# Modulation gates as columns through DRAM, grouped DMA transposes and a new order in an adaLN block

## The chip, the cores and the metric

The kernel runs on one core of one Trainium2 chip. The metric is the device time of one execution in microseconds (us). Engines are named as in the profile: PE (TensorE), PEld (its weight loads), DVE (VectorE), ACT (ScalarE), POOL (GpSimd) and SP (SyncE, which here only issues DMAs).

## The reference

One transformer block with conditioning: a linear attention with a Hedgehog feature map, and a gated feed-forward part. S = 2048 tokens, D = 512, 32 heads of 16, F = 1376; all inputs are bf16.

```python
mod = (silu(c) @ w_mod).reshape(6, 512)          # c: (1, 512), w_mod: (512, 3072)
sa, ca, ga, sb, cb, gb = mod
h = layernorm(x) * (1 + ca) + sa
q, k, v = h @ wqkv                                # 32 heads of 16
phi(t) = [softmax(t @ w_phi), softmax(-t @ w_phi)]   # 32 features a head
kv, z = phi(k).T @ v, phi(k).sum(tokens)          # per head
o = (phi(q) @ kv) / (phi(q) @ z + 1e-6)
x = x + ga * (o @ wo)
h = layernorm(x) * (1 + cb) + sb
x = x + gb * ((sigmoid(h @ w_gate) * (h @ w_up)) @ w_down)
```

The six vectors of `mod` do not depend on the token. `ga` and `gb`, the gates, scale the columns of `wo` and `w_down`.

## The kernel before, in words

The 2048 tokens are 16 tiles of 128 (t = 0 to 15). All weights and x stay in SBUF. The program is a graph of some 1200 small tasks. Each task has a name, the engines it can run on, and a function that issues its instructions. A text, `ORDER`, lists all tasks in one sequence that was searched ahead of time; `@A`, `@D`, `@P` choose ACT, DVE or POOL where the first engine given for the task is not meant. Every engine runs its tasks in the sequence of that text, and waits only for data and for buffers. Buffers are given out along the same text. PSUM has 8 banks.

The names that matter (numbers are tiles or parts):

- `ld_*`: loads, all issued by SP. `ld_wm00`, `ld_wm01`, `ld_wmga`, `ld_wmm2` load w_mod in pieces; `ld_x0a` to `ld_x3` load x.
- `c1`, `c2`, `c3`: silu(c) as a column. `warm0`, `warm1_*`: matmuls on zeros, to fill PE's early waits.
- `modc1`, `modc2` (line 723; copies at 728 and 729): shift and scale of the two LayerNorms as columns: 128 x 1 matmuls with w_mod as the weights, one for each 128 outputs and each quarter of the 512 inputs.
- `scb` (693): silu(c) spread over 128 columns. `ga`, `gb` (901): the gates as 128 equal rows, by 4 matmuls of 512 columns each. `gac` (906) and `gbc` (903): their copies out of PSUM. `wo0` to `wo3` (908) and `wd0` to `wd10` (917): the weights times the gates.
- `tpw`, `wTc`, `wqT`, `fold`, `foldc` (742 to 767): w_phi is folded into the q and k weights; `bd` (694) is the block-diagonal w_phi, and its tile is written again by `perm` (284, 287) with a permutation that `kvp` uses.
- LayerNorm 1: `st1`, `rs1`, `nmr1`, `xn1` (782 to 811) by token tile; then the transpose, in the groups of `LG`. Where `TD` is 0, `tph` (824) transposes on PE into PSUM, and `hm1` (831, 833) applies scale and shift on the way out. Where `TD` is 1, `xT1` (816) transposes by DMA into h1T, and `hm1` works in place.
- For each token tile: `K` (850) and `V` (854) project, `e` (866) takes exp of both signs, `n` (869) sums over the features, `r` (879 to 882) takes the reciprocal, `phi` (872) multiplies, `va` (890) copies v, and `kv` (274) adds to two PSUM banks over all tiles. `NPART` splits these by parts in the last tiles: `phi14.4` is the part of tile 14 from 4/8 on.
- `kvm` (295), `kvp` (310), `kvz` and `kvn` (319 to 327) turn the sums into one 128 x 144 block for each of 8 groups, kvbd. No output token can be worked on before this; it closes the first stage.
- `Q` (928), `qe` (933): the transposed query features of 4 tiles at a time; they fit in before and behind that point.
- For the output tokens: `sm`, `smS`, `den` (tiles 0 to 7) or `z` (367, 369) and `dn` (383 to 391; tiles 8 to 15): the denominators; `num` (360, 444), `u` (433 to 450), `o` (468), `oT` (471, by DMA; through PE for the first two tiles), `out` (477, with wo), `x1` (482), `st2`, `rs2`, `nmr2`, `xn2`, `xnT`, `mod` (second LayerNorm, 486 to 547).
- The feed-forward part by chunks of 1, 1, 2, 4, 4, 4 tiles: `g`, `u` with a dot (568), `tg` (tanh, 578), `hm` (589), `y` (606), `fin` (613), `st` (615, the store). `y` of tile t takes 11 matmuls, y0.0 to y0.10, and y0.k needs `wd`k. The last tile's y is cut by columns in two pieces, the second marked `b`.
- `bnd*`: a check on the size of the inputs, which chooses a general path that does not run here.

```python
LG = [[0], [1], [2, 3], [4, 5], [6, 7], [8, 9], [10, 11], [12, 13], [14, 15]]
TD = [0, 0, 0, 0, 0, 0, 1, 1, 0]
G.add("scb", {"ACT": 0.62}, lambda e: act.activation(scb[:], sc_bf[:].unsqueeze(2).to_broadcast([P, KT, P]), ACT.Copy), ...)
```

Of the kernel before, what the change touches and what calls it, by code (L numbers as in the profile page):

```python
# [22 lines left out]
NG = 8  # L23
# [7 lines left out]
LG = [[0], [1], [2, 3], [4, 5], [6, 7], [8, 9], [10, 11], [12, 13], [14, 15]]  # L31
TD = [0, 0, 0, 0, 0, 0, 1, 1, 0]
MGU = 5
LETTER = {"A": "ACT", "D": "DVE", "P": "POOL"}
ORDER = """
wdz warm0 c1 warm1_0 warm1_1 warm1_2 pmem ld_x0b st1_3 st1_2 bd c2 rs1_2 warm1_3 ld_x0a st1_0 warm1_4 warm1_5 warm1_6 rs1_0 ld_wk ld_x1 st1_1 rs1_1 warm1_7
tpw3 tpw2 wTc2 tpw0 ld_wm00 ld_wm01 wTc0 tpw1 c3 wTc3@D nmr1_2 warm1_8 warm1_9 warm1_10 warm1_11 warm1_12 warm1_13 xn1_0 nmr1_1 wTc1 fold13 foldc13 xn1_2@P
fold11 fold10 tph03 tph01 fold12 foldc10 foldc11 foldc12 xn1_1@P xn1_3@P st1_5 ld_x2 st1_4 st1_6 st1_7 modc1.0 ld_wv tph02 tph23 tph21 rs1_3@P nmr1_3 modc1.1
modc1c tph20 tph13 warm1_14 tph00 hm1_20 hm1_01@A hm1_21@A hm1_03@A hm1_13 hm1_00 hm1_02 tph22 rs1_4@P nmr1_4 K0 tph10 hm1_22@A hm1_23@A K2 ld_wq st1_11 e0.0
xn1_4@P xn1_5@P xn1_6@P hm1_10@A st1_10 tph11 st1_9 st1_8 e2.0 hm1_11@A tph12 hm1_12@A V2 xn1_7@P tph31 K3 hm1_31 e3.0 tph43 tph30 K1 tph32 rs1_6@P nmr1_6  # L40
# [8 lines left out]
n14.4 Q02 kv11.0 kv11.2 Q11 V13 ld_wg qe02 qe11 scb kv11.6 r14.4 n15.0 va13@D r15.4 n14.0 phi12.0 r14.0 r15.0 phi14.4 V14 V15 va15 va14 phi15.4 ga kv12.0
kv13.0 modc2.0 kv13.4 kv14.4 kv15.4 phi14.0 qe10 Q01 kvm1 gac kvp2 kvz2 kv14.0 phi15.0 kv15.0 qe01 Q32 kvm0 kvp1 kvp0 qe32 wo1@D wo2 kvz0 kvz1 gb kvn1@A kvn2  # L50
sm0 modc2.1 sm1 modc2c smS1 gbc kvn0 smS0@D qe13 Q12 sm2 num00 num21 num31 num01 den0 wo0 wo3 den1 Q21 qe12 smS2 wo_all wmod_free u00 u01 num11 num30 tpo0 oT0
den2 u31 u30 u11 wd4 Q31 qe31 wd0 wd2 o3 out0 num10 num20 Q23 qe21 x1_0 u10 wd7 wd1 Q30 qe23 st2_0 u21 u20 qe30 rs2_0 Q33 tpo1 sm4 smS4 nmr2_0 oT1@D xn2_0
num60 Q22 num71 qe33 den4 xnT0 out1 oT3 out3 Q20 u71 x1_1 u60 mod00@A mod02@A mod03@A mod01@A x1_3 st2_3 g0.9 g0.0 u0.9 g0.6 u0.0 o2 wd9 tsw tg0.9 tg0.0 oT2
out2 hm0.0 qe20 tg0.6 wd5 g0.5 g0.8 u0.6 wr st2_1 hm0.9 hm0.6 tg0.5 tg0.8 x1_2 u0.5 u0.7 u0.8 hm0.5 hm0.8 wd6 wd10 rs2_1 sm3 g0.1 g0.7 num61 u0.1 qe22 nmr2_1
st2_2 tg0.7 tg0.1 hm0.1 u0.4 wd3 g0.3 u0.3 tg0.3 xn2_1 g0.2 g0.10 g0.4 u61 hm0.3 hm0.7 tg0.4 tg0.2 u0.2 y0.0 rs2_2 hm0.2 nmr2_2 y0.1 xnT1 num70 o6 xn2_3@P
y0.2 y0.3 u0.10 wd8 xn2_2@P mod11 oT6 xnT3 xnT2 hm0.4 num50 y0.4 u70 smS3@D y0.5 y0.6 mod10@A tg0.10 mod13@A mod12@A u1.1 g1.1 y0.7 tg1.1 num51 g1.5 hm0.10
den3 hm1.1 g1.8 g1.9 u1.5 tg1.9 tg1.5 u51 u50 hm1.5 y0.8 y0.9 u1.8 y0.10 fin0 u1.4 g1.4 tg1.4 hm1.4 g1.0 u1.9 u1.0 num41 g1.3 num40 tg1.8 hm1.9 hm1.8 tg1.0
u1.6 u1.3 g1.2 u1.7 mod21@A tg1.3 u40 hm1.0 hm1.3 o7 mod20@A g1.6 tg1.2 tg1.6 hm1.6 u41 u1.10 g1.7 tg1.7 u1.2 o5 out6 mod22@A mod23@P g2.2 oT7 o4@D out7 x1_6
hm1.7 hm1.2 st2_6 x1_7 g2.0 g2.6 u2.0 g2.10 tg2.6 st2_7 tg2.0 st0 oT5 oT4 hm2.0 g1.10 u2.10 u2.6 tg1.10 hm2.6 hm1.10 rs2_4 nmr2_4 g2.1 u2.4 g2.4 tg2.10 hm2.10
num80 z80@D xn2_7@D tg2.4 tg2.1 hm2.4 num81 u2.1 hm2.1 num82 y1.0 out5 z81@D tg2.2 z82 dn8 x1_5 u800 y1.1 y1.2 y1.3 u2.2 hm2.2 xn2_6 xnT7 xnT6 y3.0 out4 g2.8  # L60
g2.5 u2.8 y1.4 tg2.5 y1.5 y1.6 y1.7 y1.8 y1.9 tg2.8 st2_5 x1_4 st2_4 u811 u821 hm2.8 u820 g2.7 y3.1 g2.3 u2.5 rs2_3 u2.3 mod43@A tg2.3 nmr2_3 xn2_5 xnT5 hm2.5
xn2_4@P xnT4 hm2.3 y1.10 num102 z102@D fin1 num92 tg2.7 g2.9 u2.9 num91 num90 y2.0 y2.1 y3.2 tg2.9 z91@D hm2.9 z90 z92 dn9 y3.3 y3.4 u2.7 y2.2 y3.5 y2.3 u900
u921 hm2.7 u911 mod40@P y2.4 y3.6 y2.5 num100 num101 y2.6 mod30@A z101 z100 mod31@P mod42@P mod32@P y2.7 st1 u920 num110 y2.8 y3.7 y2.9 y2.10 o9 dn10 u1021
u1000 fin2 u1011 u1020 o10 o8 y3.8 y3.9 mod33@A mod41@A g3.10 g3.8 u3.10 num130 g3.0 y3.10 tg3.10 z130 tg3.8 hm3.10 fin3 st2 oT9 u3.8 num112 hm3.8 tg3.0 z112
# [12 lines left out]
tg5.5 hm5.5 y9.8 y9.9 y9.10 u5.1 u5.0 g5.0 tg5.1 hm5.1 fin11 fin9 u5.9 u5.10 tg5.0 bndc g5.2 hm5.0 tg5.2 u5.4 g5.9 hm5.4 hm5.2 tg5.9 hm5.9 g5.10 st11 st9
tg5.10 hm5.10 bndd y13.0 y13.1 y13.2 y13.3 y12.0 y12.1 y12.2 y13.4 y13.5 y13.6 y13.7 y13.8 y13.9 y13.10 fin13 st13 y12.3 y12.4 y12.5 y12.6 y12.7 y12.8 y12.9
# [1038 lines left out]
```

## Time and profile before

| | |
|---|---|
| median of 3 runs | 210.98 us (210.16 to 211.16) |
| profiled execution | 209.63 us |
| its span, first to last instruction | 207.9 us |
| granted PE clock | 1.00 |
| PE, DVE, ACT, POOL busy | 200.3, 168.2, 107.9, 103.4 us |
| HBM read, written | 11.58 MB, 2.10 MB |
| K0 starts; last `e` ends | 13.35; 50.2 us |
| kvm1, kvm0 start | 55.3, 56.7 us |
| last matmul ends, last add starts | 204.8, 204.84 us |

The median of the runs is the time that is compared. The profile is one execution and has a time of its own; the 1.7 us between its time and its span lie around the instructions. A busy PE may be waiting inside a matmul, because the ends of pipelined matmuls are modelled. A mean duration of an instruction includes what it overlaps with the next one on its engine, so sums of durations come out larger than the time they take.

### The profile page before, as it was taken

To read this page: it belongs to the slowest core of one execution; us is meant where nothing else is said; L and a number is where in the kernel's file an instruction comes from. 1 tells how busy PE (TensorE), PEld (TensorE's weight loads), DVE (VectorE), ACT (ScalarE), POOL (GpSimd) and SP (SyncE) were. 2 spreads that over 40 slices of the span, in tenths; PEclk is the share of its full clock that TensorE was granted. 3 is DMA by queue.
4 is the path that set the end of the run, shared out by engine and by line. 5 is a ranking of instruction groups with operands and counts; after the bars stand their busy time and mean duration, and the time that the engine had idled before them with its cause. 6 is when DMAs were issued, how large, how long until landed. Compare 5 with 4: busy or idle time off the path is not lost.

```text
span 207.9 us, 4302 instructions
## 1 busy us (share of the span) xinstructions
PE 200.3 (96%) x1516; PEld 112.4 (54%) x1539; DVE 168.2 (81%) x459; ACT 107.9 (52%) x259; POOL 103.4 (50%) x137
## 2 busy tenths in 40 slices
PE   7789999999999999999999999999999999999994
PEld 2555465454675588976764544454444444444443
DVE  3999999999599998899988999979797815456642
ACT  2699999999886986524443322521244300142300
POOL 5589999999996989601337202633040612000000
PEclk9999999999999999999999999999999999999999
DMA  6995922999200201522032210342011131001011
GB/s 179 367 349 144 130 32 51 321 390 401 82 3 3 50 2 30 122 33 42 12 76 52 54 25 0 77 101 55 0 29 47 25 79 50 25 2 50 3 60 54
DMA packets 30893, 18.74 MB, mean 90 GB/s; under 512 B 20657, under 2 KB 28818, under 8 KB 30866
## 3 DMA queue, kind: packets, MB, share of 16 engines
q1 hardware_dynamic: 30336, 18.39, 31.6%
q8 instruction: 14, 0.23, 0.5%
q14 instruction: 13, 0.11, 0.2%
q10 hardware_dynamic: 530, 0.02, 0.1%
HBM read 11.58 MB, written 2.10 MB: 66 GB/s over the span
## 4 chain that ended last, share of the span: by engine, by line
PE 74%; ACT 7%; POOL 6%; DMA 4%; DVE 3%; issue 3%; SPq 1%; POOLq 0%; DVEq 0%
PE y_ps L606 18%; PE g_ps L568 17%; PE u_ps L568 17%; PE a_ps L477 6%; POOL phi L872 5%; PE q_ps L928 5%; DMA wmod_sb<-in_w_mod_dram 4%; ACT h1T L831 3%; ACT e L866 2%; DVE ks L869 2%; PE num L360 2%; PE num L444 2%; PE v_ps L854 1%; PE g_ps L570 1%; ACT tg L578 1%
## 5 line engine op out<-in xcount | busy, mean ns | idle before, releaser
L578 ACT ACTIVATE tg<-g_ps 128x512 bf16<-128x512 f32 (+4 forms) x66 | 28.7, 454 | 66.2 <-PE g_ps L568 50.5
L606 PE MATMUL y_ps<-wd_sb,wmod_sb 128*128 128x512 bf16 (+3 forms) x182 | 42.2, 366 | 0.2
L589 DVE SCALAR_TENSOR_TENSOR wmod_sb<-tg,u_ps 128x512 bf16<-128x512 bf16 (+4 forms) x63 | 30.0, 495 | 13.0 <-ACT tg L578 7.0
L872 POOL TENSOR_TENSOR phi<-e,ks 128x1024 bf16<-128x1024 bf16 (+2 forms) x22 | 31.5, 1453 | 0.5
L568 PEld LDWEIGHTS <-wu_sb 128*128 128x128 bf16 (+1 forms) x252 | 21.7, 99 | 15.4
L568 PEld LDWEIGHTS <-wg_sb 128*128 128x128 bf16 (+1 forms) x252 | 21.4, 99 | 15.2 <-issue 0.2
L606 PEld LDWEIGHTS <-wmod_sb 128*128 128x128 bf16 (+1 forms) x187 | 17.9, 98 | 16.5
L568 PE MATMUL g_ps<-wT_sb,wg_sb 128*128 128x512 bf16 (+2 forms) x121 | 23.8, 321 | 0.2
L568 PE MATMUL u_ps<-wT_sb,wu_sb 128*128 128x512 bf16 (+2 forms) x123 | 23.7, 322 | 0.1
L497 POOL TENSOR_SCALAR ve<-mv 128x2 f32<-128x2 f32 (+1 forms) x8 | 1.8, 223 | 41.2 <-DVE mv L487 41.2
L568 PE MATMUL g_ps<-wqk_sb,wg_sb 128*128 128x128 bf16 (+4 forms) x127 | 19.9, 287 | 0.1
L613 DVE TENSOR_TENSOR ot<-y_ps,x 128x512 bf16<-128x512 f32 (+1 forms) x17 | 11.1, 656 | 11.0 <-PE y_ps L606 10.5
L568 PE MATMUL u_ps<-wqk_sb,wu_sb 128*128 128x128 bf16 (+4 forms) x128 | 19.5, 287 | 0.0
L468 POOL TENSOR_TENSOR o<-u 128x512 bf16<-128x512 f32 x12 | 15.2, 1268 | 8.7 <-DVE u L435 4.7
L869 DVE TENSOR_REDUCE ks<-e 128x64 f32<-128x1024 bf16 (+2 forms) x22 | 19.4, 899 | 0.0
L866 ACT ACTIVATE e<-k_ps 128x512 bf16<-128x512 f32 (+2 forms) x44 | 18.1, 502 | 0.3 <-PE k_ps L850 0.2
L933 ACT ACTIVATE eT<-q_ps 128x512 bf16<-128x512 f32 x32 | 17.0, 622 | 1.3 <-PE q_ps L928 1.0
L850 PE MATMUL k_ps<-wqk_f,h1T 128*128 128x512 bf16 x62 | 15.8, 379 | 0.4 <-DVE h1T L833 0.3
L477 PE MATMUL a_ps<-wo_sb,oT 128*128 128x512 bf16 x61 | 15.8, 379 | 0.1
L928 PE MATMUL q_ps<-h1T,wqk_f 128*128 128x512 bf16 x58 | 15.6, 379 | 0.3
L854 PE MATMUL v_ps<-wv_sb,h1T 128*128 128x512 bf16 x62 | 15.6, 379 | 0.2
L782 DVE BATCH_NORM_STATS2 st<-x_sb 128x6 f32<-128x512 bf16 x16 | 10.7, 669 | 2.5 <-DMA x_sb<-in_A_x_dram 2.5
(158 smaller groups left out, 331.3 us busy)
## 6 DMA issues: line engine op xcount, KB each, us to landing
out_dram<-ot SPq DMA_DIRECT2D x15, 128.0 KB, 1.9
x_sb<-in_A_x_dram SPq DMA_DIRECT2D x3, 512.0 KB, 8.5
wmod_sb<-in_w_mod_dram SPq DMA_DIRECT2D x3, 512.0 KB, 7.5
wmod_sb<-in_w_mod_dram SPq DMA_DIRECT2D x1, 1536.0 KB, 14.9
wu_sb<-in_B_w_up_dram SPq DMA_DIRECT2D x1, 1376.0 KB, 9.7
wg_sb<-in_B_w_gate_dram SPq DMA_DIRECT2D x1, 1376.0 KB, 16.4
wd_sb<-in_B_w_down_dram SPq DMA_DIRECT2D x1, 1280.0 KB, 6.6
wqk_sb<-in_A_wqkv_dram SPq DMA_DIRECT2D x2, 512.0 KB, 7.6
```

Of the source, the lines that this page charges most:

```text
L477: pe.matmul(ap_[:], lhsT=oT[:, j, :], rhs=wo_sb[:, j, :], start=(j == 0), stop=(j == KT - 1))
L568: pe.matmul(ps[:fsz, 0:n], lhsT=w[:, j, ft * P:ft * P + fsz], rhs=h[:, j, 0:n], start=(j == 0), stop=(j == KT - 1))
L578: G.add(f"tg{k}.{ft}", {"ACT": 0.13 + n * 0.00083}, lambda e, tg=tg, g_ps=g_ps, fsz=fsz, n=n: act.activation(tg[:fsz, 0:n], g_ps[:fsz, 0:n ...
L589: dve.scalar_tensor_tensor(hm_all[:fsz, hm[k].slot, ft, 0:n], tg[:fsz, 0:n], 1.0, u_ps[:fsz, 0:n], op0=ALU.add, op1=ALU.mult)
L606: mm = pe.matmul(y[:, 0:c1 - c0], lhsT=hm_all[:fsz, hm[k].slot, ft, tl * P:(tl + 1) * P], rhs=wd_sb[:fsz, ft, c0:c1], start=(ft == 0), sto ...
L850: pe.matmul(kp[:], lhsT=h1T[:, j, t * P:(t + 1) * P], rhs=wqk_f[:, j, D:2 * D], start=(j == 0), stop=(j == KT - 1))
L854: pe.matmul(vp[:], lhsT=h1T[:, j, t * P:(t + 1) * P], rhs=wv_sb[:, j, :], start=(j == 0), stop=(j == KT - 1))
L866: act.activation(ee[:, ha:hb, s, :], kp[:, ha * DH:hb * DH].rearrange("p (h j) -> p h j", j=DH), ACT.Exp, scale=1.0 - 2.0 * s)
L869: dve.tensor_reduce(ks[:, ha:hb].rearrange("p h s -> p (h s)"), ee[:, ha:hb].rearrange("p h s j -> p (h s) j"), axis=AX.X, op=ALU.add)
L872: pool.tensor_tensor(ph[:, ha * 32:hb * 32].rearrange("p (h j) -> p h j", j=DH), ee[:, ha:hb].rearrange("p h s j -> p (h s) j"), ks[:, ha: ...
L928: pe.matmul(qp[:], lhsT=wqk_f[:, j, blk * P:(blk + 1) * P], rhs=h1T[:, j, cq * 512:(cq + 1) * 512], start=(j == 0), stop=(j == KT - 1))
L933: act.activation(eT[cq][:, s * 4 + blk, :], qp[:], ACT.Exp, scale=1.0 - 2.0 * s)
```

## The change

1. The gates are worked out as columns, like the shifts and scales: `modca` (16 one-column matmuls) and 16 more in `modc2`; ACT copies them to `gcol`, 128 x 8. SP writes four columns to a DRAM tensor (`gwa`, `gwb`: 512 values of 4 bytes), and reads them back as one row into all 128 partitions (`gra`, `grb`). `scb`, `ga`, `gac`, `gb`, `gbc` and their PSUM banks go.
2. LayerNorm-1 tiles 8 to 15 form two groups of four, both transposed by DMA. `xT1_8`, `9`, `14`, `15` are new, `tph5x` and `tph8x` go; `hm1` of such a group is one instruction of 512 columns for each j, and may run on DVE too.
3. `phi` may run on DVE. `z` copies 16 columns instead of 8 out of PSUM, and `dn` reads only SBUF, with 5 operations fewer.
4. `perm` writes a tile of its own (`bdp`) and no longer waits for the folds.
5. The last tile's y is cut 384 and 128 columns instead of 256 and 256.
6. `ORDER` is another text. The loads keep their sequence up to `ld_x2`; then come wq, wv, wmga, x3, and later wo and wg ahead of the last four transposes. On DVE: phi4.0, 6.0, 11.6, 13.0, 13.4, 14.0, 14.4, 15.4.

```diff
-LG = [[0], [1], [2, 3], [4, 5], [6, 7], [8, 9], [10, 11], [12, 13], [14, 15]]
-TD = [0, 0, 0, 0, 0, 0, 1, 1, 0]
+LG = [[0], [1], [2, 3], [4, 5], [6, 7], [8, 9, 10, 11], [12, 13, 14, 15]]
+TD = [0, 0, 0, 0, 0, 1, 1]
...
+bdp = cst.tile([P, KT, P], BF16, name="bdp")
+gcol = cst.tile([P, 8], FP32, name="gcol")
+gdr = [drp.tile([KT, P], FP32, name=f"gdr{i}") for i in range(2)]
...
-zS = small("smS", [P, 3, 3, 8])
+zS = small("smS", [P, NG, 16])
...
+es = [zS[:, 4 * s:4 * s + 4, 8:16] for s in range(2)]
 for s in range(2):
+    dve.tensor_tensor(m[:, 0, 32 * s:32 * s + 32]..., zS[:, 4 * s:4 * s + 4, 0:8], es[1 - s], op=ALU.mult)
+dve.tensor_tensor(den[:, 0], m[:, 0, 0:32], m[:, 0, 32:64], op=ALU.add)
+dve.reciprocal(den[:, 0], den[:, 0])
+for s in range(2):
+    dve.tensor_tensor(cc[:, 0, s]..., es[1 - s], den[:, 0]..., op=ALU.mult)
...
-steps[-2:] = [(CHUNKS[k] - 1, 0, 256), (CHUNKS[k] - 2, 0, 512), (CHUNKS[k] - 1, 256, 512)]
+steps[-2:] = [(CHUNKS[k] - 1, 0, 384), (CHUNKS[k] - 2, 0, 512), (CHUNKS[k] - 1, 384, 512)]
...
+def f_mc2(ps):
+    act.mul(gcol[:, 4:8], ps[:, 8:12], 0.5)
+    act.copy(modc[:, 8:12], ps[:, 0:4])
+    act.add(modc[:, 12:16], ps[:, 4:8], 1.0)
+modc_task("modca", list(range(8, 12)), ["wmod_ga", "wmod_ga"], ["gcola"], lambda ps: act.copy(gcol[:, 0:4], ps[:]), 0.2)
+modc_task("modc2", list(range(12, 24)), ["wmod_m2", "wmod_m2"], ["mod2", "gcolb"], f_mc2, 0.5)
...
-G.add(f"phi{t}.{a}", {"POOL": 0.08 + 1.77 * w}, f_p, ...)
+G.add(f"phi{t}.{a}", {"POOL": 0.08 + 1.77 * w, "DVE": 0.08 + 1.07 * w}, f_p, ..., port=("POOL", "DVE"))
...
-G.add("gb", {"PE": 0.87}, lambda e: f_mm(e, gb_ps, 5 * D), r=["scb", "wmod_m2"], w=["gb"], bufs=[gb_ps])
-G.add("ga", {"PE": 0.87}, lambda e: f_mm(e, ga_ps, 2 * D), r=["scb", "wmod_ga"], w=["ga"], bufs=[ga_ps])
+def f_gw(i):
+    sp.dma_start(gdr[i][:].rearrange("k p -> p k"), gcol[:, 4 * i:4 * i + 4])
+def f_gr(i):
+    sp.dma_start(gb_bc[:] if i else ga_sb[:], gdr[i][:].rearrange("k p -> (k p)").unsqueeze(0).to_broadcast([P, D]))
```

The new text around the second group's transposes and around the end of the first stage (tasks of other engines in between left out):

```
... ld_wo ld_wg n5.0 xn1_15@D ... xT1_15 phi4.0@D xn1_12@D ... xn1_13 xT1_13 V11 V8 V9 ... gwa ld_wd ... hm1_62@A ... hm1_63@A ... hm1_60@P hm1_61@P K13
... phi15.0 n14.0 r14.4 r14.0 ... phi14.0@D phi14.4@D phi15.4@D V15 perm ... kvm1 ... modc2.0 qe01 qe03 kvm0 kvp2 ... modc2.1 gra wo2 wo0 wo3 ... modc2c ... gwb ... grb
```

More of the change, by code (lines that the diff above doesn't have):

```diff
@@ L37 @@
[L37 to L40, printed above, removed]
@@ L49 @@
[L49 to L52, printed above, removed]
@@ new lines @@
+kv11.6 Q13 r15.4@A va14 qe13 V13 va13 phi14.0@D phi14.4@D phi15.4@D V15 perm Q03 kv12.0 kv13.4 kv14.4 va15 kv15.4 ld_wd2 kvm1 kv13.0 kv14.0 kv15.0 modc2.0
+qe01 qe03 kvm0 kvp2 qe11 wr kvp1 kvp0 modc2.1 gra wo2 wo0 wo3 kvz2 kvz1 kvn1@A modc2c kvn2@A kvz0 sm0 kvn0 smS0@D den0 sm2 smS2 Q30 qe32 den2 num00 qe30 wo1
+wo_all gwb num30 num01 num10 wmod_free Q12 sm1 u01 u00 qe12 smS1 num31 Q23 tpo0 grb u31 den1 u30 oT0 o3 oT3 Q31 num11 out0 u11 x1_0 u10 st2_0 qe31 num20 num21
+qe23 wd4 wd6 Q21 qe21 u20 u21 o2 sm4 oT2 smS4 rs2_0 tpo1 nmr2_0 Q33 Q20 oT1 wd9 wd1 den4 out1 x1_1 num60 num70 xn2_0 xnT0 num71 tsw u70 u60 out3 sm3 num61
@@ L692 @@
     G.add("c3", {"DVE": 0.5}, f_c3, r=["c2"], w=["scbf"], bufs=[c_ps])
-    G.add("scb", {"ACT": 0.62}, lambda e: act.activation(scb[:], sc_bf[:].unsqueeze(2).to_broadcast([P, KT, P]), ACT.Copy), r=["scbf"], w=["scb"])
     G.add("bd", {"POOL": 1.15}, lambda e: pool.tensor_tensor(
@@ L886 @@
             G.add(f"r{t}.{a}", rw, f_r, r=[("ks", t, a)], w=[("kr", t, a)], bufs=[ks])
[L887 removed]
+            G.add(f"phi{t}.{a}", {"POOL": 0.08 + 1.77 * w, "DVE": 0.08 + 1.07 * w}, f_p, r=[("kr", t, a)], w=[("phi", t, a)], bufs=[ee, ks, ph], port=("POOL", "DVE"))
         G.add(f"V{t}", {"PE": 0.87}, f_v, r=h1k + ["wv"], w=[("v", t)], bufs=[vp])
```

155 lines of the change are left out of this document (72 added, 83 removed).

## The prediction

> **What bounds the kernel now.** I read the sums of the page first.
>
> ```profile
> PE 200.3 (96%) x1516; PEld 112.4 (54%) x1539; DVE 168.2 (81%) x459; ACT 107.9 (52%) x259; POOL 103.4 (50%) x137
> ```
>
> PE's 96% says little alone, since a waiting matmul counts as busy. So I priced PE's work by spacings from the chain of waits, where back-to-back work shows what it really takes:
>
> ```profile
> 44.51 0.86 PE k_ps L850 x4
> 57.92 0.86 PE gb_ps L901 x4
> 195.26 9.56 PE y_ps L606 x55
> 204.84 0.42 DVE ot L613
> ```
>
> Four 512-column matmuls take 0.86 us. Priced so, with 0.055 for a 128-column transpose (four take 0.39 in the timeline, less the 0.22 of one alone), the PE tasks of ORDER from the first key projection `K0` (starts at 13.35) to `kvm1` (55.3) sum to 42.05 us in 41.95 us. From there to the last `y` (204.8) they sum to 147.7 in 149.5. PE has no air in the first stage and 1.8 us in the second.
>
> Then the windows (us: busy and count of PE, PEld, DVE, ACT, POOL):
>
> ```profile
> 0.00:13.30 13.30, 10.30 (x102) 5.62 (x102) 9.24 (x31) 7.85 (x20) 8.36 (x30) 1.00 0.88 290
> 13.30:45.00 31.70, 31.34 (x243) 16.77 (x249) 31.34 (x68) 31.50 (x80) 31.05 (x32) 1.00 0.67 178
> 45.00:57.20 12.20, 12.03 (x116) 6.57 (x117) 9.52 (x21) 10.62 (x26) 12.04 (x12) 1.00 0.68 262
> 80.00:130.00 50.00, 49.66 (x397) 32.18 (x402) 46.78 (x159) 18.97 (x54) 17.38 (x23) 1.00 0.22 46
> ```
>
> From 13.3 to 45, DVE, ACT and POOL are as full as PE; to 57 POOL stays full while DVE and ACT get air. From 80 to 130 DVE has only 3.2 us free and POOL is idle two thirds of the time. DVE's own waits from 45 to 58 name what closes the first stage:
>
> ```profile
> DVE kvm L295 <- POOL phi L872: 1.4, 1, 1.4
> ```
>
> **The change, part by part.** Rows used (line, form, count; busy, mean ns):
>
> ```profile
> L901 PE MATMUL gb_ps<-wmod_sb,scb 128*128 128x512 bf16 x4 | 1.0, 380 | 0.0
> L824 PE MATMUL tp_h<-ident,xn 128*128 128x128 bf16 x48 | 5.1, 218 | 0.1
> L723 PE MATMUL modc_ps<-sc_bf,wmod_sb 128*128 128x1 bf16 x64 | 2.2, 163 | 0.1
> L872 POOL TENSOR_TENSOR phi<-e,ks 128x1024 bf16<-128x1024 bf16 x12 | 23.1, 1929 | 0.4
> L908 DVE TENSOR_TENSOR wo_sb<-wo_sb,ga_sb 128x512 bf16<-128x512 bf16 x1 | 0.9, 916 | 0.0
> L450 DVE TENSOR_TENSOR u<-num,cc 128x512 f32<-128x512 f32 x12 | 7.9, 683 | 0.4 <-PE num L444 0.2
> L468 POOL TENSOR_TENSOR o<-u 128x512 bf16<-128x512 f32 x12 | 15.2, 1268 | 8.7 <-DVE u L435 4.7 <-DVE u L450 2.0 <-DVE u L433 1.5
> ```
>
> *Gates on PE.* `ga` and `gb` go: 8 matmuls at 0.216 = -1.73. Tiles 8, 9, 14, 15 lose their PE transposes: 16 at 0.055 = -0.89. Added: 32 one-column matmuls; 16 take 0.54 with 0.16 latency, so 0.025 each = +0.80. PE: **-1.82**, all where PE has no air.
>
> *Gates on ACT.* `scb` 0.72, `gac` 0.62, `gbc` 0.60 go; two copies of 0.17 come: -1.6, beside other work.
>
> *Gates by DMA.* On SP each gate is a write of 512 four-byte pieces, then a read of 2 KB into 128 partitions. No row shows such a write: between 1.9 us (small store) and 3.4 (`wp_sb`, 512 pieces of 32 B); I take 3.4, the nearest row. The read lies between 1.9 and 3.0 (`x_sb`, 256 KB). The ga pair: its read stands on SP behind the loads of wd, wu and the rest of wmod (4.3 MB, 11 us at 390 GB/s); `modc2` needs the same wmod, so it lands before PE gets there, and `wo` starts no later than its 56.3 of before. Nothing. The gb pair comes after `modc2c` (about 57.5): `wd` starts on POOL at 61.3 to 64 where it starts at 60.4 now. SP waits between the pair; behind it stands the transpose `oT3`. `out2` needs o2, behind `wd4` and `wd6`: PE reaches it at about 72, which lets `wd4` start as late as 65.5. Cover 1.5 to 4 us: I take 0; beyond it every us is a us. The Trainium skill (DMA: Bandwidth & Descriptors, Specifications) says that pieces under 512 B are read, modified and written and miss line rate; by it the write alone would lengthen, with no figure for it, and no run here shows such a write.
>
> *LayerNorm 1 in groups of four.* hm1 for tiles 8 to 15 is 8 instructions of 512 columns instead of 16 of 256. 512-column bf16 rows: ACT 0.78 (two xn1 in 1.56), POOL 0.777. The order puts 3 on ACT and 5 on POOL. SP gains four transposes at 1.2 us, and xT1_15, 14, 12, 13 queue behind wo and wg. A transpose lands in 2.4 us, 4.1 to 4.3 behind a load. xT1_13 waits for `xn1_13` on ACT (about 37.6, below), lands at 40 to 42, and K13 follows at about 42: cover 0 to 2 us, and all four tiles must land before the first modulation. I put a loss here into the ACT rival.
>
> *Moves between engines, modc1c to the end of the first stage.* I counted the tasks of both orders, at mean durations. POOL: phi 22 to 14 instructions, hm1 1 to 5, xn1 10 to 7, `perm` later: 44.1 to 32.9. DVE: +8 phi pieces (4.75 full ones), -4 va, -3 foldc, -4 hm1: 46.1 to 46.3. ACT to its last `e`: -3.8 hm1, +1.7 va, +1.7 foldc, +0.8 xn1, +1.1 qe, +0.4 smaller: 42.2 to 44.1. Overlap makes sums of durations too large: DVE's 46.1 took 43.1 less 2.2 idle, a factor 0.89; ACT 0.90.
>
> A full phi on DVE has no row: 1.15 from the reduction of the same 1024 elements (1.195 at L869), 1.83 as twice L908. I took 1.15; the difference is 2.8 us of DVE.
>
> *Startup.* The loads up to wm01 keep their places, so `modc1` still waits for 11.3. But xn1_3 stands on ACT ahead of the four fold copies: 0.78 against 0.43 idle there, `modc1c` slips from 11.97 to 12.25: **+0.28**. Moving wq ahead of wv delays wv by 512 KB (1.5 us, from 14.3 to 15.8); V1 comes at 17. The ga part of wmod ahead of the last x load puts that off as much, to about 20; its statistics come at 28. Nothing.
>
> *dn and z (second stage).* z copies 16 columns instead of 8 and dn runs from SBUF, 5 operations fewer: about -0.6 of DVE for each of 8 tiles. PE is the bound there: 0.
>
> *Tail.* The last piece is 128 columns instead of 256: the final add 0.42 becomes 0.28 (L433's form): **-0.14**; the store lands in 1.9 either way.
>
> Sum: -1.82 + 0.28 - 0.14 = -1.68. Against the profiled execution, 209.63 (span 207.9): 207.95. The median of the runs is 1.35 above it: 210.98 - 1.68 = **209.3**.
>
> **The rivals.**
>
> *More than the sum.* PE's 1.8 us of air in the second stage goes too, since DVE and POOL lose load and the order is new. For: DVE has 3.2 us free in 80 to 130 and gains 4.9. Against: a searched order has no reason to find all of it. 209.3 - 1.8 = 207.5.
>
> *ACT keeps the stage long.* ACT was full from 12.2 to 50.2 and gets 1.9 more (1.7 by the factor), and 0.28 late: its last `e` ends at 52.2. Then n14.0, two reciprocals and three phi halves on DVE (0.65 + 0.7 + 1.95): kvm1 at 55.5, as now; kvm0 at once instead of waiting for POOL, 56.5 against 57.2. PE's work behind that point is the same in both orders (145.9), so PE's saving turns into waiting: -0.65 - 0.14 = -0.8, 210.2. For: the windows. Against: three of those ACT tasks are not needed for K and e to go on.
>
> *POOL's and DVE's port (slower).* The one wo on DVE while POOL does the same work takes 0.916, against 0.683 for 512 elements with an input in PSUM. DVE now gets 48 instructions with both inputs in SBUF (8 phi, 40 in dn) where nearly all read PSUM before. Phi at twice L908: +2.8 us in a stage with 2.2 idle, most of that the wait for phi: +1.2 on the path. If each dn once waits out one `o` of POOL (1.268): 8 x 1.268 = 10.1 less the 4.9 saved = 5.2, less 3.2 free: +2.0. Together +3.2 - 1.68 = +1.5, 212.5. It decides from the point where the waits pass the idle and the saving, 2.2 + 3.2 + 1.7 = 7.1 us, 0.15 us for each of the 48; the wo row shows 0.23 under a full POOL, and POOL is a third full behind 80. The Trainium skill (SBUF — State Buffer, Who interferes with whom) says that such a DVE instruction and a POOL one that reads SBUF exclude each other for a whole instruction: by it the full 1.268 could fall on any of the 48; the row of 0.916 agrees in sign, not in size.
>
> **How the numbers follow.** About 0.5%, 1.05 us, can be told from no change here. Forecast 209.3: 0.36. More: 0.16. ACT: 0.27. Port: 0.21. Faster is the first two, 0.52; same 0.27; slower 0.21. The range runs from 207.0, below the second case, to 212.6, the port at its full price. Within the faster cases alone it is 207.0 to 209.8.
>
> **What would show it.** Right: no ga_ps and gb_ps rows, 32 transposes at tp_h's line, 96 one-column matmuls; kvm1 at 54 to 54.8; the last y about 203.1; the final add 0.28. ACT: `e` ends after 51.5 and key matmuls wait for h1T around 42. Port: phi on DVE over 1.4 for 1024 elements, dn's SBUF operations over their 0.16 to 0.35, DVE above 48 us in 80 to 130. Gates: POOL idle ahead of wd until after 65. I am wrong outright if the startup moves by more than 0.5, or if PE waits in the second stage by more than 3 us.

## The result, and the profile after

| | before | after |
|---|---|---|
| median | 210.57 us (209.77 to 211.16, 4 runs) | 225.99 us (225.23 to 228.76, 4 runs) |
| profiled execution | 209.63 us | 225.23 us |
| its span | 207.9 us | 223.5 us |
| mean granted PE clock | 1.00 | 0.97 |

The changed kernel is slower: 1.0723 times the time before (95% interval 1.0665 to 1.078), 15.4 us. All ratios leave out runs more than 1.5% above the fastest of their kernel; after the change that is the 228.76. Forecast were 209.3 us in a range up to 212.6.

The sums and the clock row of the changed kernel's page (the clock in 40 slices of 5.6 us, tenths of full speed):

```profile
PE 205.3 (92%) x1547; PEld 114.0 (51%) x1547; DVE 167.2 (75%) x422; ACT 111.7 (50%) x267; POOL 93.1 (42%) x123
PEclk9999999999857998899999999999999999999999
```

PE's share falls from 96 to 92%, and the clock, at 9 throughout before, has two dips, behind 56 and behind 84 us. The chain of waits (start, us, what) shows what stands there:

```profile
38.24 0.58 SPq L899
38.87 0.50 SPq L671
39.41 0.65 SPq L670
40.11 23.51 DMA wmod_sb<-in_w_mod_dram
63.66 0.80 PE modc_ps L716 x24
64.47 0.93 PE kvp L314 x16
65.39 0.63 PE modc_ps L716 x24
66.25 9.33 DMA gdr<-gcol
75.64 5.59 DMA wmod_sb<-gdr
81.29 2.28 POOL wd_sb L916 x2
83.57 1.23 POOL o L462
84.82 2.42 DMA oT<-o
87.28 1.89 PE a_ps L471 x4
```

Read it from the top. SP issues `gwa` (L899), then the loads of wd, wu and wmm2. wmm2 lands 23.5 us after its issue, where it took 14.9 before; only then can `modc2` start. Its gate column is written in 9.33 us and read back in 5.59; `wd4` and `wd6` wait for that, `o2` stands behind them on POOL, and PE waits for o2's transpose. The waits of PE and of POOL name the same two places (total, times, longest):

```profile
PE modc_ps L716 <- DMA wmod_sb<-in_w_mod_dram: 6.2, 1, 6.2
PE a_ps L471 <- DMA oT<-o: 4.6, 2, 3.4
POOL wd_sb L916 <- DMA wmod_sb<-gdr: 5.9, 1, 5.9
```

The windows of the changed kernel (the last three columns are PE's clock, the DMA engines' busy share, GB/s) show that the loads stand still behind the first write, what follows the first wait, and the stretch in which the second write is under way:

```profile
42.00:48.00 6.00, 6.00 (x42) 2.79 (x41) 5.63 (x15) 5.66 (x16) 5.84 (x6) 1.00 0.84 16
60.00:65.00 5.00, 1.33 (x37) 1.34 (x38) 0.18 (x1) 0.00 (x0) 0.53 (x2) 0.50 0.39 150
65.00:70.00 5.00, 5.00 (x76) 3.90 (x74) 3.73 (x13) 3.39 (x10) 4.11 (x4) 0.50 0.06 4
70.00:75.00 5.00, 5.00 (x49) 3.03 (x48) 4.13 (x10) 2.86 (x6) 0.89 (x1) 0.98 0.00 0
```

The first of these windows before the change:

```profile
42.00:48.00 6.00, 5.95 (x47) 3.03 (x46) 5.56 (x14) 5.32 (x13) 5.92 (x6) 1.00 1.06 393
```

From 42 to 48 us the DMA engines count as 84% busy and move 16 GB/s; before, they moved 393 GB/s. Busy with what, the DMA packets of the changed kernel say, from 39 to 40 us and then from 42 to 48:

```profile
DMA packets 532, 0.00 MB, mean 2 GB/s; under 512 B 532, under 2 KB 532, under 8 KB 532
DMA packets 96, 0.10 MB, mean 16 GB/s; under 512 B 0, under 2 KB 96, under 8 KB 96
```

The 512 pieces are all recorded within the first microsecond. The 96 packets behind them are of the loads, and each counts as busy for 0.84 us on average (84% of 16 engines over 6 us), where a packet of the same stretch before took 0.09. So the loads are held up behind the write: they get going between 48 and 50 us, some 10 us after its issue. The second write has no loads behind it: it is under way from 66.25 to 75.58 us, and from 70 to 75 the engines move nothing and count as idle. What a write does between its packets and its landing, the trace does not record.

After the first wait PE works at half clock: 5.00 of 5 us busy from 65 to 70, at 0.50.

### The profile page after: what moved, and what is told of

It reads as the page before. It is cut to its first block, busy times and chain, and to the rows that moved or that the text cites. A ratio compares the mean times of both kernels' runs of the same rounds, so it can differ in the third digit from the quotient of the medians.

```text
span 223.5 us, 4310 instructions
## 1 busy us (share of the span) xinstructions
PE 205.3 (92%) x1547; PEld 114.0 (51%) x1547; DVE 167.2 (75%) x422; ACT 111.7 (50%) x267; POOL 93.1 (42%) x123
## 4 chain that ended last, share of the span: by engine, by line
PE 56%; DMA 22%; ACT 12%; DVE 4%; SPq 2%; POOL 2%; issue 1%; ACTq 0%; DVEq 0%
PE u_ps L562 16%; PE g_ps L562 15%; PE y_ps L600 15%; DMA wmod_sb<-in_w_mod_dram 14%; PE a_ps L471 5%; DMA gdr<-gcol 4%; ACT e L864 4%; DMA wmod_sb<-gdr 2%; ACT h1T L829 2%; ACT vaug L888 2%; PE num L364 2%; PE g_ps L564 1%; DMA oT<-o 1%; POOL wd_sb L916 1%; ACT xn L805 1%
## 5 line engine op out<-in xcount | busy, mean ns | idle before, releaser
L572 ACT ACTIVATE tg<-g_ps 128x512 bf16<-128x512 f32 (+5 forms) x66 | 28.5, 452 | 63.3 <-PE g_ps L562 45.4
L600 PE MATMUL y_ps<-wd_sb,wmod_sb 128*128 128x512 bf16 (+4 forms) x187 | 44.1, 367 | 0.0
L562 PEld LDWEIGHTS <-wg_sb 128*128 128x128 bf16 (+1 forms) x252 | 22.0, 100 | 16.0 <-issue 1.1
L462 POOL TENSOR_TENSOR o<-u 128x512 bf16<-128x512 f32 x13 | 16.4, 1268 | 22.5 <-DVE u L427 16.3
L870 POOL TENSOR_TENSOR phi<-e,ks 128x1024 bf16<-128x1024 bf16 (+2 forms) x14 | 22.3, 1605 | 6.8 <-issue 3.0
L562 PE MATMUL g_ps<-wT_sb,wg_sb 128*128 128x512 bf16 (+2 forms) x124 | 23.5, 322 | 0.1
L562 PE MATMUL u_ps<-wT_sb,wu_sb 128*128 128x512 bf16 (+2 forms) x124 | 23.5, 322 | 0.0
L471 PE MATMUL a_ps<-wo_sb,oT 128*128 128x512 bf16 x64 | 17.3, 395 | 4.6 <-DMA oT<-o 4.6
L607 DVE TENSOR_TENSOR ot<-y_ps,x 128x512 bf16<-128x512 f32 (+2 forms) x17 | 11.2, 656 | 10.2 <-PE y_ps L600 10.2
L927 PE MATMUL q_ps<-h1T,wqk_f 128*128 128x512 bf16 x64 | 16.8, 396 | 0.0
L916 POOL TENSOR_TENSOR wd_sb<-wd_sb,wmod_sb 128x512 bf16<-128x512 bf16 x11 | 12.5, 1160 | 5.9 <-DMA wmod_sb<-gdr 5.9
L444 DVE TENSOR_TENSOR u<-num,cc 128x512 f32<-128x512 f32 (+1 forms) x16 | 10.5, 682 | 4.5 <-POOL o L462 3.2
## 6 DMA issues: line engine op xcount, KB each, us to landing
wmod_sb<-in_w_mod_dram SPq DMA_DIRECT2D x1, 1536.0 KB, 23.5
```

Of the source, the lines that this page charges most:

```text
L462: G.add(f"o{t}", {"POOL": 1.3, "DVE": 0.62}, lambda e, ub=ub, o=o: engine(e).tensor_tensor(o[:], ub[0][:].rearrange("p h d -> p (h d)"), u ...
L471: pe.matmul(ap_[:], lhsT=oT[:, j, :], rhs=wo_sb[:, j, :], start=(j == 0), stop=(j == KT - 1))
L562: pe.matmul(ps[:fsz, 0:n], lhsT=w[:, j, ft * P:ft * P + fsz], rhs=h[:, j, 0:n], start=(j == 0), stop=(j == KT - 1))
L572: G.add(f"tg{k}.{ft}", {"ACT": 0.13 + n * 0.00083}, lambda e, tg=tg, g_ps=g_ps, fsz=fsz, n=n: act.activation(tg[:fsz, 0:n], g_ps[:fsz, 0:n ...
L600: mm = pe.matmul(y[:, 0:c1 - c0], lhsT=hm_all[:fsz, hm[k].slot, ft, tl * P:(tl + 1) * P], rhs=wd_sb[:fsz, ft, c0:c1], start=(ft == 0), sto ...
L870: engine(e).tensor_tensor(ph[:, ha * 32:hb * 32].rearrange("p (h j) -> p h j", j=DH), ee[:, ha:hb].rearrange("p h s j -> p (h s) j"), ks[: ...
```

## The experiments

The theory after the result, here called *pieces*: the gate columns' 4-byte pieces cost the 15.4 us, first through the loads behind them on the queue, then through their own late landing. Its rivals: *trip* (any way through DRAM costs this), *order* (the new order and the longer first stage are the larger part) and *clock* as a share of the first loss. All ratios are to the kernel before, measured on the same chip beside each group of runs. Line numbers are those of each kernel.

**1. No DRAM.** The gates are made as in the kernel before, and `perm` writes into the tile of `bd` again (part 4 of the change goes too); all else is as changed.

```diff
-modca.0 modca.1 modcac ... gwa ... gra ... gwb ... grb
+scb ... ga ... gac ... gb ... gbc
```

> The changed kernel with the two gates as the kernel before has them: eight broadcast matmuls, two copies out of PSUM, no DRAM tensor. The new order, the LayerNorm-1 tiles by DMA in groups of four and phi on DVE stay. Theory 'pieces' (the gates' columns, each written as 512 pieces of 4 bytes, cost the 15.4 us, first by holding up the 4.3 MB of loads behind the write, then by landing late for wd): both waits go, wmm2 lands by about 52 us after its issue as before the change, PE waits under 1 us at modc2.0, and the time is 209 to 213 us. Rival 'order' (the new order and the longer first stage are the larger part: kvm1 1.8 us later, phi on DVE, modc2.0 ahead of kvp): at least half of the loss stays, 218 us or more.

212.38 us, 1.0094 (1.0057 to 1.013). PE's wait for wmod is gone. Of the 15.4 us, 13.6 went with the DRAM detour; *order* as the larger part falls. But 2.0 us stay, so the rest of the change is not free either.

**2. The write behind the loads.**

```diff
-gwa ld_wd ... ld_wu ... ld_wmm2 ... ld_wd2
+ld_wd ... ld_wu ... ld_wmm2 ... ld_wd2 gwa
```

> The changed kernel with one DMA moved: the first gate's write (gwa) stands behind the four bulk loads wd, wu, wmm2 and wd2 on SP's queue in place of ahead of them. Theory 'pieces', its part on the queue: wmm2 lands within about 15 us of its issue (23.5 us now) and PE's wait of 6.2 us at modc2.0, with the half clock after it, goes; the write itself still takes about 9 us and so the four wo products start at 65 to 70 us, and the second gate's write still lands too late for wd; so 216 to 221 us. Rival 'order': the loads are late for where the order issues them, the write's place changes nothing, 224 us or more. Rival 'trip' (what costs is the way to DRAM and back, however long the queue): wo later by what the write is later, 226 us or more.

218.88 us, 1.0398 (1.0344 to 1.0451): as *pieces* says. wmm2 lands 13.7 us after its issue and PE's wait at modc2.0 is gone. This parts the loss, within a microsecond or two: 7.1 us came from the queue, 6.7 (to the 212.17 of the next run) from the late landing. (The profiled execution began its modulation 2.2 us later than that of the changed kernel.) The chain of this kernel:

```profile
61.53 9.84 DMA gdr<-gcol
71.44 4.00 DMA wmod_sb<-gdr
```

Here the second write starts beside the read of the first gate. In the changed kernel it had nothing in front of it (0.06 busy from 65 to 70 us, 0.00 from 70 to 75) and took 9.33. So 9 to 10 us are the write's own time, not a wait behind others.

**3. The same 2 KB in 128 pieces of 16 bytes.**

```diff
-gdr = [drp.tile([KT, P], FP32, ...)]
+gdr = [drp.tile([P, KT], FP32, ...)]
-sp.dma_start(gdr[i][:].rearrange("k p -> p k"), gcol[:, 4 * i:4 * i + 4])
+sp.dma_start(gdr[i][:], gcol[:, 4 * i:4 * i + 4])
```

> The changed kernel with the DRAM tensors laid out as [128, 4] in place of [4, 128]: each gate's write is 128 pieces of 16 bytes in place of 512 of 4, the same 2 KB, at the same place of the order; the read back stays one row of 2 KB to all partitions, and the twelve-plus-four products with wd and wo read the gate with a step of 16 bytes. Theory 'pieces': the write takes 2.3 to 4 us in place of 9.3, the loads behind it are held up by a quarter, PE waits under 2 us at modc2.0, and the time is 210 to 215 us. Rival 'trip': a write to DRAM and its read cost their fixed time whatever the pieces; the write stays above 7 us and the time at 223 us or more. Rival 'order': 220 us or more with the write short.

212.17 us, 1.0083 (1.0048 to 1.0117). The DMA issues of this kernel (KB each, us from issue to landing):

```profile
gdr<-gcol SPq DMA_DIRECT2D x2, 2.0 KB, 2.5
wmod_sb<-gdr SPq DMA_DIRECT2D x1, 256.0 KB, 3.3
```

A quarter of the pieces, a quarter of the time: 2.5 us against 9.33. *Trip* falls: the way through DRAM is still there, and costs no more than the broadcast matmuls of run 1. The pieces are 13.8 of the 15.4 us (225.99 - 212.17). Their number, their size and their places in DRAM change together in this edit; which of the three sets the time is open. The number alone does not: the load of `wp_sb` has 512 pieces too, of 32 bytes, and landed in 3.4 us.

**4. The write alone, in the kernel before.** Issued ahead of its bulk loads, read by nobody; once and twice.

```diff
+G.add("xw0", {"SP": 0.5}, lambda e: sp.dma_start(xdr[0][:].rearrange("k p -> p k"), modc[:, 0:4]), r=["mod1"], ...)
-... fold01 n11.6 ld_wd2 ld_wd ld_wu ...
+... fold01 n11.6 xw0 ld_wd2 ld_wd ld_wu ...
```

> The kernel before with one thing added: a column tile of 128 x 4 float32 is written as 512 pieces of 4 bytes to a DRAM tensor that nothing reads, issued on SP's queue right ahead of the loads wd2, wd, wu, wmga and wmm2. Nothing waits for the write itself, all gates stay broadcast matmuls, the order stays. Theory 'pieces': the loads behind it are held up by 8 to 10 us, wmm2 lands at 60 to 62 us where it landed at about 52, PE waits 2 to 5 us at the second modulation or at the gates' matmuls, its clock falls behind the wait, and the time is 213 to 218 us. Rival 'order' (the write blocks loads only in the new order, or only because the program waits for it): 210 to 211.5 us.

214.47 us, 1.0204 (1.0156 to 1.0252). PE waits 2.3 us for wmod at modc2, as *pieces* has it, in an order that is otherwise untouched. wmm2 landed at 58.0 us (chain: 43.80 + 14.22), short of the 60 to 62 expected: the write was issued at 31.5 us, and 3 us of it fell into a stretch in which no load stood behind it.

> The kernel before with two of the unread writes of 512 pieces of 4 bytes ahead of the bulk loads, in place of one (214.47 us, 4.3 over the kernel before, with PE's wait at the second modulation 2.3 us). Theory 'pieces': the first write used up the loads' cover, so the second, of the same 9 us, is paid nearly whole: wmm2 lands at about 69 to 71 us, PE waits 9 to 12 us there with a slow clock behind it, and the time is 222 to 227 us. Rival (writes of one queue overlap, or it is a fixed time of the first): 214 to 217 us.

Four runs: 218.5 to 218.7 three times and 214.26 once; they fall too far apart for a ratio, so what the second write costs is open: 4 us in three executions, nothing in one. None comes near the 222 to 227 us of *pieces*: that the second write is paid nearly whole was wrong. The profiled execution is one of the three (218.72): PE waits 3.7 us for wmod at `ga` and 1.3 at modc2, and its clock is 0.50 from 55.2 to 65.4 us; in the execution of 214.26 the granted clock was 1.00. The windows of this kernel and then of the one with one write, at the point where the loads get going:

```profile
42.00:44.00 2.00, 1.95 (x25) 1.11 (x25) 2.00 (x5) 1.57 (x3) 1.92 (x2) 1.00 0.31 22
```

```profile
42.00:44.00 2.00, 1.55 (x15) 0.83 (x15) 1.97 (x6) 2.00 (x5) 1.92 (x2) 1.00 0.70 162
```

With two writes wmm2 lands at 60.5 us, 2.5 later than with one, so two writes in a row overlap in large part. How, no run here shows.

**5. The clock.** 28 matmuls ahead of modc2.0 fill the first wait.

```diff
-... kv15.0 modc2.0 ...
+... kv15.0 warm2_0 ... warm2_27 modc2.0 ...
```

> The changed kernel (225.99 us) with 28 matmuls of 512 columns put into PE's order right ahead of modc2.0, 6.1 us of work at full clock whose results nothing reads; they fill the wait for wmm2. Theory 'clock' (about 3 us of the first loss is not the wait but the half clock that PE ran at from 62 to 70 us after it): PE is busy until modc2.0, the granted clock stays at 0.9 or more from 60 to 70 us, and the time is 222 to 224 us. Rival: the slow clock has another cause, or the second gate's late landing swallows what is won: 225.5 us or more; if the filling only delays modc2.0, 226.5 us or more.

224.21 us, 1.066 (1.0601 to 1.0719), 1.8 below the changed kernel and just above the expected 222 to 224. The interval overlaps that of the changed kernel, so the gain in time is not clear of the noise; the clock is read from the trace. Its windows:

```profile
63.70:70.00 6.30, 6.30 (x123) 4.81 (x120) 5.50 (x17) 4.47 (x13) 4.54 (x4) 1.00 0.04 0
85.00:90.00 5.00, 4.56 (x31) 3.51 (x32) 2.01 (x6) 0.55 (x2) 4.55 (x6) 0.50 0.28 54
```

With PE kept busy the clock stays at 1.00 behind the wait, so the slow stretch there came from the wait itself. The second wait came 2 us earlier and its slow stretch grew, from 3.4 us in the changed kernel (87.2 to 90.6) to 6.8 (84.0 to 90.8): part of the gain was given back.

**6. What is left: phi on DVE.** In run 3, the phi of DVE and of POOL by form from 44 to 58 us (last columns: busy us, mean ns, idle before), then ACT's wait:

```profile
L870 DVE TENSOR_TENSOR phi<-e,ks 128x512 bf16<-128x512 bf16 x5 | 5.0, 1044 | 0.1
L870 POOL TENSOR_TENSOR phi<-e,ks 128x1024 bf16<-128x1024 bf16 x3 | 6.1, 2017 | 0.6 <-ACT ks L878 0.5
```

```profile
ACT e L864 <- DVE phi L870: 1.4, 1, 1.4
```

The median of DVE's phi in that kernel is 0.72 us, but one of 512 elements took 2.41, beside a POOL phi that took 2.20 instead of 1.93. The next exponentials waited 1.4 us for the buffer. So:

```diff
-... phi11.6@D phi13.0@D phi13.4@D ...
+... phi11.6 phi13.0 phi13.4 ...
```

> The kernel with 16-byte pieces (212.17 us) and three phi of tile 11 and 13 (phi11.6, phi13.0, phi13.4) moved from DVE back to POOL. In that kernel's trace one 512-element phi on DVE took 2.41 us where the median of its kind is 0.72, beside a phi of 2.19 us on POOL (1.93 alone), ACT's next exponentials waited 1.45 us for the buffer that it held, and POOL was idle 2.35 us right after. Theory 'port' (what is left of the loss, 1.8 us, is DVE's phi waiting for POOL's): no phi on DVE over 1 us, ACT's wait under 0.5 us, kvm 1 to 1.5 us earlier (56 to 56.5 us), and 210.7 to 211.4 us. Rival 'ACT' (ACT's work sets the end of the first stage): kvm within 0.5 us of 57.5, 211.8 us or more. Rival 'POOL': its three longer phi (0.62 and two of 1.05 us) make kvm later, 212.5 us or more.

210.31 us, 0.9998 (0.9978 to 1.0018). By form in the same stretch of this kernel:

```profile
L869 DVE TENSOR_TENSOR phi<-e,ks 128x512 bf16<-128x512 bf16 x3 | 2.2, 772 | 0.1
L869 POOL TENSOR_TENSOR phi<-e,ks 128x1024 bf16<-128x1024 bf16 x3 | 5.8, 1929 | 0.1
```

POOL is back at 1.93, kvm1 starts at 56.4 in place of 57.5, and 1.9 us are gone: three small instructions on the engine that is faster at them had cost that. The time is a little below the 210.7 to 211.4 us expected. With pieces and phi mended the changed kernel equals the one before. The Trainium skill (SBUF — State Buffer, Who interferes with whom) says that a DVE instruction with two SBUF inputs and a POOL one that reads SBUF exclude each other for a whole instruction. The trace of run 3 agrees: POOL's phi ran from 49.40 to 51.60 us, DVE's from 49.74 to 52.14, so it began behind POOL's and ended 0.54 after it, less than the 0.72 it takes otherwise.

The other direction, on the kernel of run 8:

> The kernel of 209.34 us with its last five phi on DVE (phi4.0, phi6.0, phi14.0, phi14.4, phi15.4) on POOL too, so that all phi are where the kernel before has them. They took 1.22 (twice) and 0.68 to 0.94 us on DVE and would take 1.93 (twice) and 1.05 (three times) on POOL. Theory 'port' says that phi on DVE costs where POOL has one at the same time: if these five still collide, kvm comes earlier and the time is 209.2 us or less. Rival 'POOL bound': POOL's 7 us more of work come late in a stage where it has 16.7 of 20 us to do, kvm comes 1 to 3 us later, and the time is 210 to 212 us; then phi on DVE is right where POOL doesn't run one.

212.45 us, 1.0082 (1.0048 to 1.0116), a little above what 'POOL bound' expected. In its profiled execution (214.22 us) kvm1 comes at 59.3, after a wait of 4.0 us for POOL's `perm`. The five phi that stay on DVE are worth 2.6 us by the ratios. Which phi goes where matters more than how many.

**7. Gates without DRAM by another way**: each column repeated as weights, the identity as the moving tile.

```diff
+pe.matmul(ps[:, j * P:(j + 1) * P], lhsT=gcol[:, 4 * i + j:4 * i + j + 1].to_broadcast([P, P]), rhs=ident[:], start=True, stop=True)
```

> The changed kernel with its gate columns (in bfloat16) spread by TensorE in place of DRAM: for each block of 128 one matmul whose weights are the column repeated 128 times and whose moving tile is the identity, then a copy out of PSUM as before the change. PE has the 32 one-column matmuls (0.80 us by the sum of the prediction) and eight of 128 columns (about 0.06 each, 0.5 us) in place of eight of 512 (1.73 us). Theory 'pieces': no wait at modc2.0, 208 to 212 us, and 0.2 to 0.6 us under the kernel with the gates by broadcast matmuls. Rival 'order': 217 us or more.

215.12 us, 1.0237 (1.0182 to 1.0292): a miss by 3 us. gb stood in PE's order right behind modc2 and waited 1.5 us for ACT to copy the column; the clock from 60 to 65 us fell to 0.66.

> The kernel with gates spread by the identity on TensorE (215.12 us), with two edits: the second gate's four matmuls and its copy stand ten tasks later (behind Q30 and its exponential), and the same three phi go to POOL. In its trace PE waited 1.5 us at those matmuls for ACT's gate column and ran at a clock of 0.66 from 60 to 65 us. If that wait and the slow stretch behind it are the 2.9 us by which it is over the kernels with broadcast matmuls and 16-byte pieces, the time falls by about 3 us for the place and by what the phi bring, to 210.5 to 212 us; with theory 'port' 1 us of it is the phi. If the identity matmuls cost more in themselves (219 ns each in the trace, not 60), 213 us or more.

212.59 us, 1.0126 (1.0088 to 1.0164): 2.5 less, not enough. Of the 2.7 us that are left over run 6 by the ratios, 1.5 have a line, in PE's waits from 100 us on:

```profile
PE u_ps L559 <- DVE u L426: 1.5, 1, 1.5
```

My reading, which no run tests: PSUM banks are given out along the order, and two more users shift who gets which, so near 147 us a u of the feed-forward part gets a bank that a late DVE task still reads. The wait is in both kernels with the identity, and not in those of runs 1, 3 and 6.

**8. Where the predicted 1.7 us went.** Run 1 with the three phi on POOL leaves the change without its gates and without `bdp`: the order, the LayerNorm groups, five phi on DVE, dn and the tail:

> The kernel with broadcast-matmul gates in the new order (212.38 us) and the same three phi moved to POOL as in the kernel with 16-byte pieces. What is then left of the change is the order, the LayerNorm-1 tiles in groups of four and five phi on DVE. By theory 'port' the move is worth here what it was there, 1.8 us: 210.2 to 211 us. The gates on PE cost 0.9 us more than as columns by the prediction's sum; if that shows, it is 0.3 to 0.9 us above the kernel with 16-byte pieces and phi on POOL (210.31 us), if the products' strided reads there cost as much, equal to it. Rival 'ACT': 211.8 us or more.

211.98 us, 1.0066 (1.0041 to 1.0091), in the range that rival 'ACT' named (211.8 or more) and not in that of 'port'. The gain of the phi was 0.6 us here by the ratios, against 1.8 in run 6, and why is not shown; its profiled execution began the modulation 0.8 us later than that of run 6. In run 6 itself the stepped read cost POOL: its products with wo took 1.42 us each. So the step was moved into the weights:

```diff
-pe.matmul(ps[:, i:i + 1], lhsT=wmod_sb[:, j, ch * P:(ch + 1) * P], ...)
+pe.matmul(ps[:, i:i + 1], lhsT=wmod_sb[:, j, c0 + ch % 4:c0 + D:4], ...)   # gate columns only
```

> The kernel with 16-byte pieces and phi on POOL (210.31 us), but the gates' one-column matmuls take every fourth weight column, so that the 16-byte pieces lie in DRAM in the gate's own order and the products with wo and wd read their gate row without a step. In that kernel's trace a product took 1.39 to 1.40 us on POOL where it took 1.16 with a plain row, four of them stand on the chain ahead of the first a_ps and eleven follow. Theory: products at 1.16 us, wo done 0.9 us earlier, PE's waits for wo and wd (0.7 us there) gone, and 209.2 to 210 us, below the kernel before. Rival: the strided weights load slower (32 of them) and give it back, or the products' time was hidden: 210.2 us or more.

**209.34 us**, 0.9956 (0.9932 to 0.9979): the best kernel of the study, 0.9 us under the one before by the ratio. The wo products by form, of run 6 and then of this kernel:

```profile
L906 POOL TENSOR_TENSOR wo_sb<-wo_sb,ga_sb 128x512 bf16<-128x512 bf16 x4 | 5.5, 1422 | 2.3 <-DMA ga_sb<-gdr 2.3
```

```profile
L908 POOL TENSOR_TENSOR wo_sb<-wo_sb,ga_sb 128x512 bf16<-128x512 bf16 x4 | 4.5, 1164 | 2.3 <-DMA ga_sb<-gdr 2.3
```

Then the gates alone, in the old order:

> The kernel before, in its own order, with one part of the change alone and in its mended form: both gates as columns (one-column matmuls that take every fourth weight column), written as 128 pieces of 16 bytes and read back as a plain row. For that the load of the first gate's weights stands behind that of wo, the second modulation is followed at once by its copies and by the second write, and wo1 goes from DVE to POOL, so that DVE doesn't wait for the first gate; LayerNorm 1 and phi stay as before. The same gates in the new order (with the three phi on POOL) gave 209.34 us, 1.0 under the kernel before. Theory: the gates are where the gain is (0.9 us of PE by the prediction's sum), and the new order with its LayerNorm-1 groups brings nothing: 209 to 210 us. Rival 'order': groups and order brought the gain: 210.2 to 211 us. Rival 'landing': in this order the gate rows land 2 to 3 us later than the copies out of PSUM did, wo's and wd's products and POOL's o behind them are late, and PE waits: 211.5 us or more.

215.12 us, 1.0234 (1.0191 to 1.0277), spoilt by its placing: PE waited 1.5 us at 22.6 us for the first gate's weights, and the first stage ended 3.8 us late. One edit later:

```diff
-... modca.0 modca.1 modcac K5 ...
+... modca.0 modca.1 modcac K8 ...
```

> The kernel before with the gates as columns in 16-byte pieces, as in the run that gave 215.12 us, with one edit: the first gate's columns (modca) stand ahead of K8 in PE's order in place of ahead of K5. In that run's trace PE waited 1.5 us for their weights at 22.6 us, the next LayerNorm-1 transposes were issued 3.4 us later than in the kernel before, and kvm came at 59.1 us where it came at 55.3: the placing cost, so the part was not tried fairly. If that stall is all that was wrong: kvm at 55.5 to 56.5 us and 209 to 210.5 us, and then order and LayerNorm-1 groups brought nothing to the 209.34 us of the best kernel. Rival 'order': 210.5 to 211.5 us. Rival 'landing' (gate rows later than the copies out of PSUM, wo and wd products and POOL's o behind them): 211.5 us or more, with DVE's u or den ahead of PE's waits after 60 us.

212.02 us, 1.0065 (1.0035 to 1.0095). Its first stage is sound (kvm1 at 56.3 with a startup 0.9 us later than before), and its chain goes through the landing:

```profile
59.26 3.28 DMA wmod_sb<-gdr
62.70 2.29 POOL wd_sb L926 x2
```

`wd` starts at 62.7 where it started at 60.4, ahead of POOL's other work, as that rival said. PE's one wait above 1 us that the kernel before does not have (1.1, for ACT's `tg` at 89.5) stands behind a `wd` product on POOL in the chain. So neither part gains alone: by the ratios, the change without gate columns gives +1.4 us, the gates in the old order +1.4, both together -0.9. That the columns pay only in an order that leaves room for their landing is my reading of that chain; no run takes the landing away in the old order.

## Why the prediction was wrong

**The step that failed is *Gates by DMA*.** I took 3.4 us for the write, "the nearest row", from `wp_sb`, a load of 512 pieces of 32 bytes. The write took 9.33 us, the read 5.59 where I had at most 3.0. Two statements rested on that. "Nothing" for the ga pair looked only at its read, queued behind the loads; the 4.3 MB of loads queued behind its write, and I never priced that direction (7.1 us, run 2). "Cover 1.5 to 4 us: I take 0; beyond it every us is a us" for the gb pair was the right rule with the wrong sizes: with `modc2c` done at 66.2 us in place of 57.5, 66.2 + 9.3 + 5.6 gives 81.1 and `wd` started at 81.29, 15.8 us beyond the 65.5 that PE could bear. 207.95 + 15.8 = 223.7, and the profiled execution took 225.23.

The sentence on the Trainium skill (DMA: Bandwidth & Descriptors, Specifications) stood beside this: pieces under 512 B are read, modified and written and miss line rate. The trace agrees as to the rate, 2 KB in 9.33 us; whether the pieces are read and modified, it does not record. The sentence spoke against this part, and I let a row of loads set the size. No bound above 3.4 stood in the range for an operation that no row showed. What the runs showed in its place: a write of 9.33 us that holds up whatever is queued behind it, with a cost of 13.8 us in all (run 3).

**The PE sum.** The counts were right: no ga_ps and gb_ps rows, 32 transposes, 96 one-column matmuls. Not all of them stood where PE has no air, though: `gb` started at 57.92, behind kvm1 (55.3), in the stage with 1.8 us of air. And that they become time was wrong: kvm1 came at 57.10 us in place of 54 to 54.8, and at 55.8 in the best kernel. Part of PE's saving in the first stage turned into waiting there: from 13.3 to 55.8 us PE was idle for 0.5 us before and for 1.1 in the best kernel. Of -1.68 the best kernel shows -0.9.

**Startup and tail** were right: modc1c at 12.34 (forecast 12.25), the last add 0.29 us (0.28).

**The port rival** had the right mechanism. Its first half, phi beside POOL, was priced at +1.2 us and measured 1.9 in run 6 and 0.6 in run 8, though it falls on one instruction and on the buffer that ACT waits for, not evenly on all eight. Its second half, eight dn that each wait out an `o`, did not occur: in the changed kernel dn's operations take 0.19 to 0.35 us on average, and DVE from 80 to 130 us stands at 46.4 in run 6, where 46.8 stood before and over 48 was the sign. I put the whole rival at 0.21 and took its full price as the end of the range.

**The ACT rival** named 52.2 for the last `e` and 210.2 us. Run 6, with both causes mended, has 52.4 and 210.31. But its last `e` waited 0.8 us for a buffer of POOL's phi, so ACT's own load is not shown to be the reason.

"Wrong outright if PE waits in the second stage by more than 3 us": it waited 6.2 at modc2 and 4.6 for oT.

## What to carry to other kernels

Before a small DMA goes ahead of bulk loads, look at its pieces, not its bytes, and ask what is queued behind it: a write to DRAM of 512 pieces of 4 bytes held the queue for about as long as 3.6 MB of loads take (9.3 us at 390 GB/s). A row in the other direction, with larger pieces, is no price for it. If a layout must be turned, turn it where it is free, here by which weight column each matmul takes. And when a faster engine is given work beside a slower one, look at the longest instance in the trace, not the median: in run 6, three of some 420 DVE instructions held 1.9 us.

## What the runs showed of the hardware that I had not expected

- The time of the write went with its pieces: 128 of 16 bytes 2.5 us, 512 of 4 bytes 9.3 to 9.8 us, the same 2 KB, also on an empty queue. In the changed kernel the 512 packets are recorded within a microsecond. For the rest of the write the DMA engines show nothing where the queue is empty (0.00 busy from 70 to 75 us), and where loads stand behind it they show those loads' packets, 0.84 us each in place of 0.09.
- PE's clock fell to 0.50 some 2.5 us into an idle stretch (57.4 to 59.9) and stayed there for 6.5 us of work after it (63.7 to 70.15), four 512-column matmuls spanning 1.87 us in place of 1.03; behind the second wait it was 3.4 us. By the clock records, the half-clock stretches inside the traces come in whole steps of 3.41 us: 10.24 and 3.41 in the changed kernel, 6.8 in run 5, 3.41 behind the wait in the first kernel of run 7. The Trainium skill (TensorE: Matmul & The Clock Gate, What's actually happening) gives about 3.4 us of sustained work until the full clock. The second stretch agrees, the first took nearly twice as long. Of its first 64 matmuls 48 had one column; whether that is why, no run shows.
- A one-column matmul whose weights are every fourth column of the tile showed no cost that could be told: the kernel with them is the fastest.
- The startup moves from execution to execution: the first copies of the modulation started between 11.7 and 12.9 us in kernels whose first loads are the same, and at 14.5 in run 2, whose PE was at half clock from 8.2 to 11.6 us. That is about as much as the gain that was looked for.
